# Four staging tiles for the first eight quarters of V, and six warm-up matmuls in place of eight

## The chip, the cores and the metric

One core of one Trainium2 chip. The metric is device time of one execution in microseconds (us). A run's span in the profile is about 1.7 us shorter than its time. "PE" is TensorE, "ACT" ScalarE, "DVE" VectorE, "POOL" GpSimd, "SP" the queue that issues most loads. In these traces PE runs at one of two clocks: 512-column matmuls start 0.427 us apart (the first ones of the kernel before) or 0.216 us apart (its later ones), called half clock or cold, and full clock or warm, below. The change to full clock is called the grant of the clock.

## The reference, cut to what matters

Two independent parts write the two halves of the output. Part A is a state-space layer (a complex scan over 2048 steps, 1024 states). Part B is attention over segments of 32 tokens with an 8-token memory. Only the first stage of the kernel is touched here, in which PE turns part B's input x, and multiplies it by Wv:

```python
h = jnp.concatenate([mem, xs], axis=1)          # part B, per segment
v = jnp.einsum('btd,dhe->bhte', h, Wv)          # 32 heads of 128
Bu = jnp.einsum('bld,pd->blp', x + 0j, B_bar)   # part A, "stage 1"
```

## The kernel before

PE is pinned to program order. It starts with eight matmuls on a zeroed tile, whose results are not used ("warm-ups"), while x is on its way from HBM:

```python
def warm(k, pool):
    w = pool.tile([128, 512], BF16, name="a_n", bufs=1)
    k.V.memset(w[:], 0.0)
    p = k.ps("R")
    for _ in range(8):
        k.PE.matmul(p[:], w[:, 0:128], w[:], start=True, stop=True)
```

The first quarter of V needs x turned by PE in four blocks of 128 tokens (`turn_x0`, eight 128-column transposes each, followed by a copy on DVE or ACT); the order is turn 0, turn 1, thirty-two 128-column matmuls, turn 2, and so on. Each later quarter of V is 4 x 8 matmuls of 512 columns into the three `psP` banks (tiles named ps are those that matmuls write to). ACT copies each bank into a staging tile, and when four are there, one DMA stores the tile:

```python
    def stage_init(self):
        self.vst = []
        for i in range(2):
            self.vst.append(self.wl.tile([128, 4, 4, EW], BF16, name=f"b_vst{i}", bufs=1))
            self.k.G.memset(self.vst[i][:, :, :, E:EW], 1.0)
        self.nst = 0

    def next_st(self):
        self.nst += 1
        return self.vst[self.nst % 2]

    def v_x(self, hb, q, w):
        st = self.next_st()
        # ... (first quarter: the turns and the small matmuls)
        for i in range(4):
            p = k.ps("P")[:]
            self.v_mm(p, w, 4 * q + i)
            k.copy("v" if first and i % 2 else "s", st[:, i, :, 0:E], p.rearrange("p (h e) -> p h e", h=4))
        Q.dma_start(vx[s0:s0 + n * 128, :]..., st[:, 0:n, :, :]...)      # Q = ACT's queue
```

So the copies of a quarter must wait for the store of the last quarter but one. After four quarters, "stage 1" of part A (psU<-a_xT,a_bt) is interleaved with the other quarters. `CT` is a large tile that is loaded only in stage 1's second half.

## Time and profile before

| | before |
|---|---|
| time, median of 3 | 1248.03 us (1247.3 to 1248.12) |
| span of the profiled run | 1246.5 us |
| PE busy | 1238.4 us, 99% |
| first stage-1 matmul | 36.19 us |

From the page of the kernel before (busy time of PE, and shares of the chain of waits that ended last):

```profile
span 1246.5 us, 20192 instructions
...
PE 1238.4 (99%) x8342; PEld 662.2 (53%) x8342; DVE 668.1 (54%) x1246; ACT 263.4 (21%) x631; POOL 276.5 (22%) x412
...
PE 97%; DMA 2%; ACT 1%; issue 0%; POOL 0%; DVE 0%; SPq 0%; ACTq 0%
```

PE bounds everything; a gain must be a stretch in which PE stands still or works slowly. Such stretches are read from the starts of matmuls, not from their durations: here 512-column matmuls are listed with some 0.38 us each, yet they start 0.216 us apart once warm.

The PE timeline of the kernel before; the columns are start, duration of the group, engine, line, operation, output<-inputs, count, and in brackets idle time before it and what ended it:

```profile
1.28 3.59 PE L64 MATMUL psR<-a_n 128*128 128x512 bf16 x8 [1.28 <-DVE hpb L105]
4.67 0.81 PE L64 MATMUL psU<-ident,b_xr 128*128 128x128 bf16 x8
5.93 0.62 PE L64 MATMUL psU<-ident,b_xr 128*128 128x128 bf16 x8 [0.45 <-DMA b_xr<-in_B_x_dram]
6.39 1.06 PE L64 MATMUL psP<-b_wv,b_xe 128*128 128x128 bf16 x16
7.67 1.07 PE L64 MATMUL psP<-b_wv,b_xe 128*128 128x128 bf16 x16 [0.22 <-ACT b_xe L89]
...
14.84 0.18 PE L64 MATMUL psR<-ident,a_r 24*128 24x24 bf16 x1
...
36.19 3.62 PE L64 MATMUL psU<-a_xT,a_bt 128*128 128x512 bf16 x16
```

The eight warm-ups take (4.67 - 1.28) / 8 = 0.42 us each, double the warm spacing: the array runs at half clock. The second turn waits for its load until 5.93. The single matmul at 14.84 ("a_r") ends this opening. From there to the first stage-1 matmul PE has only V matmuls.

The chain of waits of the kernel before, in order of time (start, duration, what), runs over ACT from 18.81 to 25.51 us and then over one store:

```profile
25.51 8.22 DMA b_vx<-b_vst
...
33.82 0.61 ACT b_vst L89
34.42 0.04 issue
34.47 1.89 PE psP L64 x8
```

and this is the copy that waits for that store, in the ACT timeline:

```profile
33.82 1.09 ACT L89 ACTIVATE b_vst<-psP 128x512 bf16<-128x512 f32 x2 [3.09 <-DMA b_vx<-b_vst]
```

The store of the second quarter takes 8.22 us, ACT stands 3.09 us, and PE, which has three banks to fill, at last waits too: two matmuls in a row start at 33.97 and 34.47, 0.498 us apart in place of 0.216.

### The profile page before, as it was taken

The page shows a single profiled execution, that of the slowest core. Times are in us where ns is not written, and L with a number is a line of the kernel's source. Part 1 is how long each engine was busy: PE and PEld are TensorE (multiplying, and loading weights), DVE is VectorE, ACT ScalarE, POOL GpSimd, SP SyncE. Part 2 cuts the span into 40 slices and gives each one's busy share as a digit, 9 for nine tenths or more (in the row PEclk, how much of TensorE's full clock was granted, in tenths as well). Part 3 has the DMA queues.
Part 4 walks back from the last instruction along what each step waited for, and adds up shares of the span by engine and source line. Part 5 has one row for each costly group of instructions (what it writes and reads, how often), then busy time and mean ns, then how long its engine had stood idle before and what let it go on. Part 6 is the DMA issues. An engine that isn't in the chain of part 4 may idle for free.

```text
span 1246.5 us, 20192 instructions
## 1 busy us (share of the span) xinstructions
PE 1238.4 (99%) x8342; PEld 662.2 (53%) x8342; DVE 668.1 (54%) x1246; ACT 263.4 (21%) x631; POOL 276.5 (22%) x412
## 2 busy tenths in 40 slices
PE   9999999999999999999999999999999999999998
PEld 4444444444455555656666656555665554446444
DVE  4688899998711124666666666666666641001000
ACT  5344444443310000211111111111211110000000
POOL 4111331212322321322222222222222220000000
PEclk9999999999999999999999999999999999999999
DMA  9975444554898734665454544545473279407000
GB/s 236 267 205 150 130 131 128 144 156 108 240 322 248 250 116 94 182 176 122 96 144 108 144 108 113 138 91 133 97 155 95 60 222 225 107 18 153 17 17 27
DMA packets 316023, 176.83 MB, mean 142 GB/s; under 512 B 138651, under 2 KB 301327, under 8 KB 315927
## 3 DMA queue, kind: packets, MB, share of 16 engines
q1 hardware_dynamic: 293830, 147.95, 48.4%
q10 hardware_dynamic: 21072, 24.38, 5.8%
q0 software_dynamic: 1024, 3.17, 0.7%
q8 instruction: 66, 1.08, 0.4%
q14 instruction: 31, 0.25, 0.1%
HBM read 89.14 MB, written 53.17 MB: 114 GB/s over the span
## 4 chain that ended last, share of the span: by engine, by line
PE 97%; DMA 2%; ACT 1%; issue 0%; POOL 0%; DVE 0%; SPq 0%; ACTq 0%
PE psP L64 81%; PE psU L64 9%; PE psS L64 3%; PE psO L64 2%; PE psR L64 2%; DMA wo<-in_B_Wo_dram 1%; DMA b_vx<-b_vst 1%; DMA b_xr<-in_B_x_dram 0%; ACT b_vst L89 0%; ACT L187 0%; ACT b_xe L89 0%; POOL b_m L643 0%; ACT a_fr L236 0%; ACT a_k L233 0%; ACT a_k L229 0%
## 5 line engine op out<-in xcount | busy, mean ns | idle before, releaser
L64 PE MATMUL psP<-b_xe,b_wq 128*128 128x480 bf16 (+1 forms) x1280 | 247.7, 343 | 0.0
L64 PE MATMUL psP<-b_xe,b_wk 128*128 128x480 bf16 (+1 forms) x1280 | 247.7, 343 | 0.0
L64 PE MATMUL psP<-b_wv,b_xe 128*128 128x512 bf16 (+2 forms) x1048 | 224.6, 372 | 0.3 <-ACT b_xe L89 0.2
L643 POOL TENSOR_TENSOR b_m<-b_e,maskB 99x396 bf16<-99x396 bf16 x160 | 139.6, 872 | 334.8 <-ACT b_e L640 334.8
L640 ACT ACTIVATE b_e<-psS 99x396 bf16<-99x396 f32 x176 | 88.2, 501 | 532.8 <-PE psS L64 528.5
L64 PEld LDWEIGHTS <-b_wk 128*128 128x128 bf16 x1280 | 119.4, 98 | 94.2
L64 PEld LDWEIGHTS <-b_xe 128*128 128x128 bf16 x1056 | 101.9, 98 | 119.4 <-issue 0.6
L64 PEld LDWEIGHTS <-b_wq 128*128 128x128 bf16 x1280 | 118.7, 98 | 87.7
L91 DVE CAST b_k<-psP 128x480 bf16<-128x480 f32 (+1 forms) x192 | 98.2, 533 | 100.9 <-PE psP L64 100.9
L91 DVE CAST b_q<-psP 128x480 bf16<-128x480 f32 (+1 forms) x192 | 98.2, 533 | 93.1 <-PE psP L64 91.5
L64 PEld LDWEIGHTS <-b_ol 128*128 128x128 bf16 x864 | 84.3, 98 | 94.4
L64 PE MATMUL psU<-a_xT,a_bt 128*128 128x512 bf16 x512 | 114.9, 379 | 0.0
L64 PE MATMUL psP<-t,a_hl 128*128 128x512 bf16 x512 | 113.1, 379 | 0.0
L91 DVE CAST b_ost<-psP 128x512 bf16<-128x512 f32 (+1 forms) x17 | 11.5, 676 | 183.4 <-PE psP L64 183.4
L64 PE MATMUL psP<-wo,b_ol 128*128 128x512 bf16 (+1 forms) x448 | 92.5, 364 | 0.0
L64 PE MATMUL psP<-t,b_ol 128*128 128x512 bf16 x416 | 92.2, 379 | 0.0
L280 POOL TENSOR_SCALAR a_tt<-a_pr,a_tabf 128x1 f32<-128x1 f32 x48 | 34.1, 710 | 243.5 <-DVE a_pr L275 243.5
L660 DVE TENSOR_TENSOR b_ob<-psO,b_accR 99x384 bf16<-99x384 f32 x160 | 85.9, 553 | 2.5 <-DVE b_accR L659 0.3
L89 ACT ACTIVATE b_vst<-psP 128x512 bf16<-128x512 f32 x126 | 72.1, 589 | 71.4 <-PE psP L64 60.3
L267 DVE TENSOR_TENSOR a_pr<-psU,a_tabf 128x2048 f32<-128x2048 f32 x32 | 73.0, 2283 | 14.8 <-PE psU L64 14.7
L64 PEld LDWEIGHTS <-a_bt 128*128 128x128 bf16 x512 | 49.2, 98 | 57.6
L64 PEld LDWEIGHTS <-a_hl 128*128 128x128 bf16 x512 | 49.0, 98 | 56.7
(199 smaller groups left out, 964.2 us busy)
## 6 DMA issues: line engine op xcount, KB each, us to landing
b_v<-b_vx SPq DMA_DIRECT2D x16, 1122.0 KB
b_wv<-in_B_Wv_dram SPq DMA_DIRECT2D x16, 1024.0 KB
b_on<-b_ob SPq DMA_DIRECT2D x15, 960.0 KB
b_vx<-b_vst ACTq DMA_DIRECT2D x24, 544.0 KB
a_hs<-a_h SPq DMA_DIRECT2D x32, 256.0 KB
b_wog<-in_B_Wo_dram SPq DMA_DIRECT2D x4, 2048.0 KB
b_wq<-in_B_Wq_dram SPq DMA_DIRECT2D x16, 512.0 KB
b_wk<-in_B_Wk_dram SPq DMA_DIRECT2D x16, 512.0 KB
```

The source lines that it names most:

```text
L64: r = f(*a, **kw)
L89: self.S.activation(out, in_, ACT.Copy)
L91: self.V.tensor_copy(out, in_)
L267: V.tensor_tensor(pr[:], u[:].unsqueeze(1).to_broadcast([128, 2, 2, TB]), view(t3, [[TB + 1, 2], [TB + 1, 2], [1, TB]]), ALU.mult)
L280: G.tensor_scalar(tt[:, j:j + 1], w[:, j, TB - 1:TB], t3[:, 1, TB:TB + 1], None, ALU.mult)
L640: k.S.activation(e[:], s[0:GW], ACT.Exp, scale=float(E) ** -0.5, accum_out=self.accE[0:GW, i:i + 1])
L643: k.G.tensor_tensor(m[0:GW, 0:4 * GW].rearrange("p (a b q) -> p a b q", a=2, b=2), e[:], mask[0:GW, :, :].unsqueeze(2).to_broadcast([GW, 2 ...
L660: V.tensor_tensor(self.ob[:, b0:b0 + n, :], o[0:GW, 0:n, 0:E], r.unsqueeze(2).to_broadcast([GW, n, E]), ALU.mult)
```

## The change

Intent: two further staging tiles in the space of `CT` that is not loaded yet, so that the first eight quarters do not wait for stores; and two warm-up matmuls fewer, since PE seems to warm up longer than x takes to arrive (the warm-ups run to 4.67 us; the DMA of the first block of x releases a weight load at 4.37).

```diff
-    def stage_init(self):
-        self.vst = []
-        for i in range(2):
-            self.vst.append(self.wl.tile([128, 4, 4, EW], BF16, name=f"b_vst{i}", bufs=1))
-            self.k.G.memset(self.vst[i][:, :, :, E:EW], 1.0)
+    def stage_init(self, ct):
+        self.vst = [self.wl.tile([128, 4, 4, EW], BF16, name=f"b_vst{i}", bufs=1)[:] for i in range(2)]
+        spare = [ct[:, 1, 4 * i:4 * i + 3, :].rearrange("p c d -> p (c d)")[:, 0:16 * EW].rearrange("p (i h e) -> p i h e", i=4, h=4)
+                 for i in range(2)]
+        self.sts = self.vst + spare
+        for st in self.sts:
+            self.k.G.memset(st[:, :, :, E:EW], 1.0)
         self.nst = 0
     def next_st(self):
         self.nst += 1
-        return self.vst[self.nst % 2]
+        return self.sts[self.nst % (4 if self.nst < 8 else 2)]
@@ def warm
-    for _ in range(8):
+    for _ in range(6):
         k.PE.matmul(p[:], w[:, 0:128], w[:], start=True, stop=True)
```

(Left out: the call `b.stage_init(a.CT)` and a `[:]` that moved.) The order of instructions on ACT, DVE and SP is the same in both kernels; POOL has two memsets more.

More of the change, by code (lines that the diff above doesn't have):

```diff
@@ L728, in load_o_early @@
         elif q == 2:
-            t = [v[:].rearrange("p i h e -> p (i h e)")[:, 0:2048].rearrange("p (h n) -> p h n", h=4) for v in self.vst]
+            t = [v.rearrange("p i h e -> p (i h e)")[:, 0:2048].rearrange("p (h n) -> p h n", h=4) for v in self.vst]
         else:
@@ L1008, in kernel_main @@
             b.load_m0(p1)
-            b.stage_init()
+            b.stage_init(a.CT)
             order = steps()
```

## The prediction

> **What bounds the kernel.** TensorE. The page gives PE 99% busy of a 1246.5 us span; the chain of waits is 97% PE. So the change can only pay where PE really stands still early on. From start-to-start distances in the PE timeline (a warm 512-column matmul is paced at 0.216 us) I find before 120 us just these losses: eight cold warm-up matmuls (1.28 to 4.67 us, 0.427 us each), a wait until 5.93 for the second block of x (PE waits, DMA b_xr), a wait until 7.67 for an ACT copy of x^T (0.39), and one distance of 0.498 us at 34.0, an excess of 0.285 us.
>
> **Staging tiles.** With two tiles, ACT's fourth quarter of V waits for the second quarter's store: the chain shows DMA b_vx<-b_vst from 25.51 to 33.73 (8.2 us), and the ACT timeline an idle of 3.09 us before the copy at 33.82. In the ACT group of b_vst the DMA ends 9.6 us of idle in 3 waits; another, 4.18 us, ends at 73.05. Only the first reaches PE: at 34.19 it wants a psP bank that ACT has not emptied, until 34.47. With four tiles that copy needs no store still in flight. The instruction order on ACT, DVE and SP is unchanged. So 0.285 us is gained, on the critical path, and kept: PE is paced by its own matmuls afterwards. The other ACT waits (about 6.5 us) are off the path. Added: two POOL memsets, 0.21 us each, near 5 us, ahead of an iota that DVE uses at 6.1: free. The transposed loads into CT come after 150 us, when the stores from its spare space have landed: free.
>
> **Two warm-up matmuls fewer.** They take 0.85 us, but PE then waits for data anyway. The weight load of the first transpose starts at 4.37, released by the DMA; so the first transposes could start near 4.45 instead of 4.67. That is not kept: the second ones wait for their DMA until 5.93. Gain 0. Risk: the clock. Transposes go from 0.107 to 0.056 us apart at 5.05 us, 3.77 us after PE started. [...] With six, PE is idle about 0.5 us before the first transposes; [...] the second transposes run at 0.107, delaying the ACT copy and PE by about 0.4 us. I give this one run in four: 0.1 us on average.
>
> **Sum.** 1248.03 - 0.285 + 0.1 = 1247.8 us, 0.02% faster, less than the spread of the three runs before (1247.3 to 1248.12). Range 1246.8 to 1248.8. Chances: faster by over 2% 0.003, within 2% 0.994, slower 0.003.
>
> **What would show it.** Right: ACT's 3.09 us wait gone, DMA b_vx gone from the early chain; PE's distance at 34 back to 0.216; first stage-1 matmuls near 35.9 instead of 36.19; second transposes still at 5.93 behind DMA b_xr, and 0.056 apart. Wrong: stage 1 still starts at 36.2 or later, cold transposes after 5.93, or a new wait for a store or for a_xT.
>
> **What would make it wrong.** A cold clock into the 128-column matmuls (0.5 us or more); x arriving earlier, so that fewer warm-ups pay 0.2 us or more; or a later load-bound place (8.47 us of DMA wo in the chain near 1007) absorbing the 0.285 us.

## The result, and the profile after

| | before | after |
|---|---|---|
| time, median of 4 | 1247.91 us (1247.3 to 1248.12) | 1248.89 us (1247.89 to 1249.14) |
| span of the profiled run | 1246.5 us | 1247.4 us |
| a_r matmul | 14.84 us | 16.30 us |
| first stage-1 matmul | 36.19 us | 37.37 us |

The ratio is 1.0007, 95% interval 0.999 to 1.0025: the same within 2%. (Ratios are the mean time of one kernel's fast runs over that of the other's of the same rounds, so not quite the ratio of the medians.) The four runs after were 1249.11, 1249.14, 1248.67 and 1247.89: three long, one short.

The page of the kernel after:

```profile
span 1247.4 us, 20115 instructions
...
PE 1236.0 (99%) x8268; PEld 663.4 (53%) x8340; DVE 668.2 (54%) x1246; ACT 263.5 (21%) x631; POOL 276.3 (22%) x414
...
PEclk9999999999999999999999999999999999999999
...
PE 98%; issue 0%; DMA 0%; POOL 0%; ACT 0%; DVE 0%; SPq 0%; ACTq 0%
```

The page says almost nothing: 8268 matmuls are 74 fewer than before, but only two were taken away; the others are records missing from the trace (the weight loads, PEld, are 8340 against 8342), which is also why PE's busy sum fell. Its clock row (PEclk, 9 is 90% or more) shows full speed in all 40 slices, and its mean clock is 0.999, although 128-column matmuls start 0.107 us apart until 10.3 us. The PE timeline of the kernel after tells more:

```profile
1.28 2.74 PE L64 MATMUL psR<-a_n 128*128 128x512 bf16 x6 [1.28 <-DVE hpb L105]
4.12 1.03 PE L64 MATMUL psU<-ident,b_xr 128*128 128x128 bf16 x8
5.68 1.03 PE L64 MATMUL psU<-ident,b_xr 128*128 128x128 bf16 x8 [0.53 <-DMA b_xr<-in_B_x_dram]
6.51 3.62 PE L64 MATMUL psP<-b_wv,b_xe 128*128 128x128 bf16 x32
9.92 0.80 PE L64 MATMUL psU<-ident,b_xr 128*128 128x128 bf16 x8
...
16.30 0.18 PE L64 MATMUL psR<-ident,a_r 24*128 24x24 bf16 x1
...
37.37 3.62 PE L64 MATMUL psU<-a_xT,a_bt 128*128 128x512 bf16 x16
```

The reader should look at the groups of 32 (after) and 16 + 16 (before) small V matmuls. Before, 32 take from 6.39 to 8.57 with a wait of 0.39 us within; after, 32 take from 6.51 to 9.92 with no wait: (9.92 - 6.51) / 32 = 0.107 us each against 0.056. The second turn takes 1.03 us in place of 0.62. PE is at half clock until about 10.3 us; before, until about 5.1.

The chain of waits of the kernel after has no store in its first 45 us:

```profile
1.28 4.36 DMA b_xr<-in_B_x_dram
...
5.68 1.03 PE psU L64 x8
6.72 3.41 PE psP L64 x32
...
22.23 10.77 PE psP L64 x49
```

and the ACT copy that had waited 3.09 us waits for PE alone:

```profile
32.39 0.60 ACT L89 ACTIVATE b_vst<-psP 128x512 bf16<-128x512 f32 x1 [0.20 <-PE psP L64]
```

So the span's +0.95 us (1247.42 - 1246.47) is: +1.46 up to the a_r matmul, -0.28 from there to stage 1 (21.35 us before, 21.07 after), and -0.23 over the remaining 1210 us, where both run the same work.

### The profile page after: what moved, and what is told of

Read it like the earlier page. It is cut to its first block, busy times and chain, and to the rows that moved or that the text cites. A ratio compares the mean times of both kernels' runs of the same rounds, so it can differ in the third digit from the quotient of the medians.

```text
span 1247.4 us, 20115 instructions
## 1 busy us (share of the span) xinstructions
PE 1236.0 (99%) x8268; PEld 663.4 (53%) x8340; DVE 668.2 (54%) x1246; ACT 263.5 (21%) x631; POOL 276.3 (22%) x414
## 3 DMA queue, kind: packets, MB, share of 16 engines
q0 software_dynamic: 1024, 3.17, 0.7%
## 4 chain that ended last, share of the span: by engine, by line
PE 98%; issue 0%; DMA 0%; POOL 0%; ACT 0%; DVE 0%; SPq 0%; ACTq 0%
PE psP L64 82%; PE psU L64 9%; PE psS L64 3%; PE psO L64 2%; PE psR L64 2%; DMA b_xr<-in_B_x_dram 0%; POOL b_m L645 0%; ACT b_e L642 0%; DVE b_ost L91 0%; SPq L64 0%; ACTq L89 0%; ACTq L642 0%
## 5 line engine op out<-in xcount | busy, mean ns | idle before, releaser
L89 ACT ACTIVATE b_vst<-psP 128x512 bf16<-128x512 f32 x110 | 62.9, 588 | 61.2 <-PE psP L64 57.8
```

What stands on the lines that cost most here:

```text
L89: self.S.activation(out, in_, ACT.Copy)
```

## The experiments

Theory ("window"): the staging tiles gain their 0.28 us; with six warm-ups PE idles long enough between 3.8 and 5.7 us that the full clock is granted late. Rivals: the space in CT costs something ("staging"); or the moment of the clock is luck and strikes both kernels alike ("chance").

The clock in the table below is from the trace's record of clock changes, which turn out to lie whole multiples of 3.413 us apart in these traces (from the grant to the next change 1239.04 us before, 363 of them, and 1235.63 after, 362); a "window" is such a stretch. The activity of a window is worked out from the PE timeline: each matmul counts from its start with 0.427 us per 512 columns (cold) or half of that (warm); what of this lies inside the window is summed and divided by 3.413 us. "Window before" is the 3.413 us ahead of the window that ended with the grant. Each line is one profiled run, for the clock was seen in profiled runs alone. From the first stage-1 matmul to the end all fourteen traces took 1209.86 to 1210.56 us (mean 1210.21, standard deviation 0.19), so larger differences between traces lie ahead of stage 1.

| run | warm-ups / tiles | clock granted, us | activity of window before | of the granting window | a_r, us | a_r to stage 1, us | that run, us |
|---|---|---|---|---|---|---|---|
| before | 8 / 2 | 5.08 | 11% | 100% | 14.84 | 21.35 | 1248.16 |
| after | 6 / 4 | 10.31 | 71% | 100% | 16.30 | 21.07 | 1249.11 |
| e1 | 8 / 4 | 4.10 | 0% | 83% | 14.76 | 21.07 | 1247.60 |
| e2 | 6 / 2 | 9.28 | 71% | 100% | 15.82 | 21.07 | 1248.88 |
| e3 | 6 / 4 | 4.06 | 0% | 78% | 14.38 | 21.07 | 1247.28 |
| e4 | 8 + fill / 4 | 6.86 | 64% | 100% | 15.32 | 21.07 | 1248.30 |
| e5 | 8 / 2 | 6.81 | 63% | 94% | 14.98 | 21.07 | 1247.70 |
| e6 | 8 / 2 | 4.75 | 2% | 100% | 14.89 | 21.60 | 1248.67 |
| e7 | 4 / 4 | 8.88 | 52% | 95% | 15.61 | 21.07 | 1248.45 |
| e8 | 6 + fill / 4 | 6.91 | 66% | 89% | 14.97 | 21.07 | 1248.15 |
| e9 | 8 / 4 | 5.33 | 20% | 100% | 14.57 | 21.07 | 1247.42 |
| e10 | 8 short / 4 | 3.93 | 0% | 75% | 14.84 | 21.07 | 1248.27 |
| e11 | 8 / 1 | 5.37 | 21% | 100% | 14.85 | 30.81 | 1257.65 |
| e12 | 8 / 4 | 7.30 | 77% | 82% | 15.40 | 21.07 | 1248.57 |

### e1: staging alone

```diff
 # the changed kernel, with
-    for _ in range(6):
+    for _ in range(8):
```

> Four staging tiles, but all eight warm-up matmuls. Clock theory (six warm-ups leave PE idle long enough that the clock is granted late; the staging tiles gain 0.28 us by themselves): clock granted near 5 us, the a_r matmul near 14.8 us, first stage-1 matmul near 35.9 us, time 0.3 us below before. Staging rival (the spare space in CT costs time, the warm-ups do nothing): about 1 us slower than before. Chance rival (the moment of the clock is luck in every kernel): spread of about 1.2 us like the changed kernel's, mean within 0.3 us of before.

Measured: 1247.6 us median (1247.39 to 1248.47, 5 runs), before 1247.54 (1247.47 to 1248.19, 9 runs), ratio 1.0001. Clock at 4.10, stage 1 at 35.83. The staging rival falls: with CT and eight warm-ups nothing is 1 us slower. The chance rival, that both kernels are struck alike, is not borne out by these five runs: none is as long as the long ones of the change (the count over all runs is below). But the gain of 0.3 us did not show in the time; e9 and e12 return to it.

### e2: fewer warm-ups alone

```diff
 # the kernel before, with
-    for _ in range(8):
+    for _ in range(6):
```

> Six warm-up matmuls, but two staging tiles as before. Clock theory: in most runs the clock is granted only near 8 to 10 us, the a_r matmul at up to 16.3 us; time 0.5 to 1.5 us above before, and the wait for the store is smaller or gone, since a late PE gives the store time. Staging rival: same as before within 0.2 us. Chance rival: same mean as before, single runs up to 1.5 us longer in both.

Measured: 1249.1 us median (1247.47 to 1249.72, 5 runs), before 1247.54, ratio 1.001. Four of five runs are at 1248.88 or more. The clock came at 9.28, the a_r matmul at 15.82. The whole loss is in this part of the change. The distance from a_r to stage 1 is 21.07 although there are only two tiles: PE came so late that the store was done (the ACT copy at 31.91 us waits 0.20 us, for PE). That also means that with six warm-ups the two parts of the change are not worth their sum: where the clock was late, as in this trace, four tiles had nothing left to save.

### e3: the changed kernel again

> The changed kernel once more, for the spread of its runs and a second look at the clock. Clock theory: most runs 0.8 to 1.2 us above before, a few as fast as before minus 0.3; the profile's clock is granted late (8 to 10 us) if its run is a long one and early (5 to 7 us) if it is a short one. Staging rival: always about 1 us longer, also with an early clock. Chance rival: mean equal to before.

Measured: 1247.28, 1248.83, 1248.89, 1247.52 and 1249.25 us; before 1247.54. The profile fell on the shortest. Its PE timeline:

```profile
1.28 2.74 PE L64 MATMUL psR<-a_n 128*128 128x512 bf16 x6 [1.28 <-DVE hpb L105]
3.97 0.65 PE L64 MATMUL psU<-ident,b_xr 128*128 128x128 bf16 x8
5.55 0.62 PE L64 MATMUL psU<-ident,b_xr 128*128 128x128 bf16 x8 [0.93 <-DMA b_xr<-in_B_x_dram]
6.00 1.06 PE L64 MATMUL psP<-b_wv,b_xe 128*128 128x128 bf16 x16
```

The same program, and here the first turn already runs warm (0.65 us; 1.03 in the first trace), with the clock granted at 4.06. So the kernel has two outcomes: in the nine runs of it, six at 1248.67 to 1249.25 (mean 1248.98) and three at 1247.28 to 1247.89 (mean 1247.56), 1.4 us apart. Early clock with a short run, late clock with a long one, is what the window theory said; of these nine runs the clock was seen in two.

### e4: eight warm-ups, and the wait for x filled

```diff
 # the kernel of e1, and in v_x
             self.turn_x0(0)
+            for _ in range(6):
+                k.PE.matmul(p0[:, 0:128], w0[:, 0:128], w0[:, 0:128], start=True, stop=True)
             self.turn_x0(1)
```

(`w0`, `p0` are the warm-up's operand and bank.)

> Four staging tiles, eight warm-ups, and six 128-column matmuls more between the first and the second transposes, where PE waits for x. Clock theory: no idle stretch of PE over 0.2 us before 6 us, [...] the clock is granted by 8.1 us at the latest in every run, the spread of runs is the smallest of all, time at or below that of e1 (0.3 us under before). Staging rival: about 1 us slower than before, as all with CT. Chance rival: same spread as before.

Measured: 1248.19 us median (1247.5 to 1248.35, 5 runs), before 1247.54. The clock came by 8.1, at 6.86; but neither the smallest spread nor a time under e1 was seen: a miss. In the profiled run the cold fill (0.64 us) kept PE busy until 6.16, where the second turn then started; in e1 it started at 5.66.

### e5 and e6: the kernel before, two more traces

No edit.

> The kernel before, as it is, for a second trace of it: is the wait at PE near 34 us (0.285 us for a bank that ACT has not emptied) in every run of it? Store theory [...]: the wait is there whenever the a_r matmul comes at 14.8 us or earlier, from 0.1 to 0.7 us, the distance from the a_r matmul to the first stage-1 matmul being over 21.07 us by just that. Rival (the wait of the first trace was luck): no wait, distance 21.07 us, so that four staging tiles gain nothing in most runs. Clock granted between 4.0 and 7.4 us.

> The kernel before, a third trace, for the same question as e5: under the store theory a wait of 0.1 to 0.7 us near 34 us if the a_r matmul comes by 14.8 us, under its rival none.

Measured: e5 1247.6 us median of 4 (1247.46 to 1248.15), before 1247.92; e6 a single 1248.67 us. The ACT copies that wait for the second quarter's store, e5:

```profile
32.71 1.08 ACT L89 ACTIVATE b_vst<-psP 128x512 bf16<-128x512 f32 x2 [1.83 <-DMA b_vx<-b_vst]
```

and e6:

```profile
34.12 1.08 ACT L89 ACTIVATE b_vst<-psP 128x512 bf16<-128x512 f32 x2 [3.34 <-DMA b_vx<-b_vst]
```

With the copy at 32.71 PE loses nothing (21.07 us from a_r to stage 1), with 34.12 it loses 0.54 (21.60), and with 33.82, in the first trace, 0.28. The wait at PE is real, but it is not in every run: when that store lands differs by over 1 us between runs of one program. My store theory said "whenever the a_r matmul comes at 14.8 us or earlier"; e5's came at 14.98 and so decides nothing between it and its rival, e6's came at 14.89 and shows the wait. Both clocks are within 4.0 to 7.4.

### e7: four warm-ups

```diff
 # the changed kernel, with
-    for _ in range(6):
+    for _ in range(4):
```

> Four warm-up matmuls and four staging tiles. Window theory [...]: PE is active from 1.28 to 2.99 and from 4.1 to 4.9, [...] the clock comes between 7.2 and 10.7 us in every run, all runs are over 1248.0 us, their median 1 to 1.7 us over before. Rival (the clock comes late by chance, or only the number of runs matters): some runs as short as before.

Measured: 1248.65 us median (1248.45 to 1250.1, 5 runs), before 1247.92 (1247.09 to 1248.18). Clock at 8.88, after a window of 52%. All runs are over 1248.0, as the window theory said; the median's +0.73 us is under the 1 to 1.7 that I gave, the mean's is 1249.04 - 1247.67 = 1.37. With four, no run is short; with six some are; with eight nearly all.

### e8: six warm-ups, and the wait for x filled

```diff
 # the changed kernel (six warm-ups), and in v_x
             self.turn_x0(0)
+            for _ in range(6):
+                k.PE.matmul(p0[:, 0:128], w0[:, 0:128], w0[:, 0:128], start=True, stop=True)
             self.turn_x0(1)
```

> The changed kernel (six warm-ups, four tiles) and six 128-column matmuls more between the first and the second transposes, where PE waits for x: 0.64 us of cold work put into the idle stretch, nothing else. Window theory: [...] the clock comes between 4.1 and 7.5 us, no run is as long as the long runs of the changed kernel (none over 1248.6 us), median within 0.3 us of before. Rival (what matters is the number of matmuls ahead of the first transposes, or the first transposes starting early): as the changed kernel, half the runs or more at 1248.7 to 1249.3 us.

Measured: 1248.15 us median (1247.63 to 1248.57, 5 runs), before 1247.92. The PE timeline of e8:

```profile
4.13 1.03 PE L64 MATMUL psU<-ident,b_xr 128*128 128x128 bf16 x8
4.96 0.84 PE L64 MATMUL psR<-a_n 128*128 128x128 bf16 x6
5.72 1.04 PE L64 MATMUL psU<-ident,b_xr 128*128 128x128 bf16 x8
6.55 2.39 PE L64 MATMUL psP<-b_wv,b_xe 128*128 128x128 bf16 x32
```

By luck this trace and that of the kernel after are a pair, for their windows lie almost alike. The windows that end at 3.50 us (e8) and 3.48 us (after) were 66% and 65% active, and gave no clock. In the next one the kernel after was 71% active, and got no clock at 6.89; e8, with the six matmuls in the gap, was 89% active and got it at 6.91. The fill is all that differs between the two programs. As expected no run was over 1248.6, if only just.

### e9 and e12: staging alone, for its gain

The kernel of e1, unchanged.

> Eight warm-ups and four staging tiles once more (the kernel of e1), because e1 could not tell a gain of 0.3 us from none. Two traces of before showed a wait of 0.28 and 0.54 us for the store, one showed none. Store theory: mean of the runs 0.1 to 0.4 us below before; distance from the a_r matmul to the first stage-1 matmul 21.07 us. Rival (the saved wait is given back later): same mean as before within 0.1 us, although the distance is 21.07 us. Window theory: no run over 1248.6 us.

> The kernel of e1 and e9 a third time, on the same terms as e9: store theory 0.1 to 0.4 us below before in the mean of all fifteen runs, its rival no difference within 0.1 us.

Measured: e9 1247.42 us median (1247.28 to 1247.45, 5 runs), e12 1247.57 (1247.45 to 1248.57, 5 runs), before 1247.72 (1247.16 to 1248.09, 9 runs of the same chip). All fifteen runs of this kernel have a mean of 1247.63, all 36 runs of the kernel before (e5 and e6 among them) 1247.73: 0.10 us, with a standard error of about 0.12 (standard deviations 0.39 and 0.36). The distance was 21.07 in all three traces. The saving at PE is seen in the traces: of those whose a_r matmul came before 14.9 us, the two with two tiles (before, e6) have the wait, the four with four tiles (e1, e3, e9, e10) have not. The rival "given back later" finds no support: from stage 1 to the end the three traces of before took 1210.20 us in the mean, those of e1, e9 and e12 1210.19. A gain in the time is not shown, 0.1 to 0.3 us remain possible. No run was over 1248.6, e12's longest only just under it: there the first window, begun at 0.48 us, before PE started, was 77% active and gave no clock, which came at 7.30.

### e10: eight warm-ups as short as six

```diff
 # the kernel of e1, with
-        k.PE.matmul(p[:], w[:, 0:128], w[:], start=True, stop=True)
+        k.PE.matmul(p[:, 0:384], w[:, 0:128], w[:, 0:384], start=True, stop=True)
```

> Eight warm-up matmuls of 384 columns and four staging tiles: as many matmuls as before, as much PE time (2.56 us cold) as six of 512 columns. Window theory: as the changed kernel; half the runs or more at 1248.6 to 1249.5 us with the clock at 8 to 10.7 us, the others at 1247.2 to 1248.0. Rival (the number of matmuls counts): as e1, no run over 1248.5 us.

Measured: 1248.27, 1247.13, 1247.46, 1248.82 and 1248.01 us; before 1247.72. One run is clearly long, where I expected half or more, and the profiled run of 1248.27 had its clock early (3.93), so that it is long for another reason. A miss for the window theory's number; between "time" and "number of matmuls" the run does not decide. That the number alone does not do it is seen in e8, which has six ahead of the first turn and no long run.

### e11: one staging tile

```diff
 # the kernel before, with
-        return self.vst[self.nst % 2]
+        return self.vst[1 if self.nst < 8 else self.nst % 2]
```

> Eight warm-ups and only one staging tile for the first seven quarters of V: the suspected wait made larger. Each quarter's first copy then waits for the quarter just before it to be stored (some 4 to 8 us), while three psP banks hold PE for 5.2 us. Store theory: PE stands still several times between 20 and 75 us, 3 to 15 us in all, and the whole is longer by that. Rival (the store waits are hidden by the other work, PE hardly sees them): under 1 us longer.

Measured: 1257.08 us median (1256.12 to 1259.51, 4 runs), before 1247.72, ratio 1.0078. PE's matmuls are late by 1.16, 2.64, 1.16 and 3.17 us near 21, 25, 33 and 43 us, 8.1 us together. The rival (hidden waits) falls. The rest of the 9.74 us by which the distance from a_r to stage 1 grew (30.81 against 21.07), 1.6 us, fits the clock, which was lost once more: half of the 3.40 us at clock 0.50 in the view below is 1.7. The windows view of e11, cut along multiples of 3.413 us; columns are the stretch, its length, PE's busy time and matmuls, the granted clock, DMA share and GB/s:

```profile
22.44:25.84 3.40, 0.96 (x5) 1.00 1.09 244
25.86:29.26 3.40, 3.38 (x9) 0.50 1.14 231
29.27:32.67 3.40, 3.40 (x17) 1.00 1.24 281
39.50:42.92 3.42, 1.44 (x7) 1.00 1.18 311
42.93:46.33 3.40, 2.39 (x12) 1.00 1.06 194
```

After a window with PE busy 0.96 of 3.40 us the clock is 0.50 for exactly one window, in which PE is busy all the time; then it is 1.00 again. A window with 1.44 of 3.42 did not lose it. The length of the idle stretch alone does not order the two: it was 2.48 us ahead of the matmul at 25.88, where the clock was lost, and 3.00 us ahead of the one at 43.94, where it was not.

## Why the prediction was right or wrong

- "TensorE bounds, 0.02% faster, within 2%": right that nothing moves by 2%, wrong in sign (four runs alone, with 0.999 to 1.0025, do not settle the sign; the nine runs of the kernel, mean 1248.51, against 1247.73 for before do). The median, 1248.89, is 0.09 us above the top of my range (1248.8), the point was 1.1 us too low. The second set of five runs gave 1248.83.
- "0.285 us is gained, on the critical path": the trace after has 21.07 us in place of 21.35, and its chain has lost its store; but e2, with two tiles and a late clock, has 21.07 too, so that trace does not show what the tiles did. The traces with an early a_r matmul (under e9 and e12) do. What was wrong is that I took one trace for every run: in three traces of before the wait was 0.28, 0 and 0.54. Over all runs staging is worth 0.10 us, standard error 0.12.
- "Two warm-up matmuls fewer: gain 0": right. The first turn came at 4.12 in place of 4.67, and the second waited for its load until 5.68.
- The step that failed is the risk of the clock: "the second transposes run at 0.107, delaying the ACT copy and PE by about 0.4 us. I give this one run in four: 0.1 us on average." That the clock could come late was right (10.31 us after, 5.08 before), both factors were not; one in four was my estimate, which no trace had shown. How often: of the fourteen runs with six full warm-ups (after, e2, e3) ten were long (1248.67 or more), of the 51 with eight full ones and at least two tiles (36 of before, 15 of e1, e9, e12) one, e6's, whose clock came at 4.75 and which was long by other things (below). e10, whose warm-ups took as much PE time as six, had one of five, so the share is known only roughly. How much: long and short runs of those fourteen differ by 1249.08 - 1247.54 = 1.54 us. I had counted only the second turn as cold. But in the trace after no clock came at the end of the window at 6.89; it came 3.41 us later, at 10.31, and everything up to there ran at half clock: the second turn, all 32 small V matmuls and a part of the third turn, with no wait left to hide it (before, PE stood 0.39 us at 7.67). With the clock from 8.88 to 9.28 and 10.31 the a_r matmul went from 15.61 to 15.82 and 16.30, about half a microsecond for each one. In these traces a grant by 5.4 us costs little (a_r at 14.4 to 14.9), since PE waits for x until about 5.7 anyway; one at 6.8 to 7.3 (a_r at 15.0 to 15.4) costs up to 0.6 us.
- Why six and not eight: in all fourteen traces the clock changes are whole multiples of 3.4133 us apart (362, 363 or 364 of them from the grant to the drop at the end; 6, then 1, then 359 in e11), and the grant fell anywhere from 3.9 to 10.3 us. With six warm-ups PE idles from 3.81 to 4.12 and from 4.95 to 5.68, 1.0 us (after), and a window that holds both is 71% active: no clock, twice seen (after, e2). With eight, only the gap ahead of the second turn is left, and windows that lie wholly after PE's start were 94 to 100% active, but for e12's, 82%: clock in every trace. At nearly the same place as in the kernel after, e5 (eight warm-ups, window ended at 6.81) was 94% active and got the clock. My reading is that the position of the windows decides which runs are long; that was not shown, for no run could choose it, and in unprofiled runs it was not seen. Measured: with six 10 of 14 were long, with eight 1 of 51; with four all five took 1248.45 us or more, though three of them less than 1248.67.
- Left open: what decides whether a window is followed by the clock. In these traces windows of 52 to 71% gave no clock in six (after, e2, e4, e5, e7, e8), those of 78% and more always did; between them, 75% did (e10) and 77% did not (e12), so the activity as counted here does not settle it. The profiled runs of e6 and e10 show that a time alone does not tell of a late clock: with the clock at 4.75 and 3.93 they took 1248.67 and 1248.27. In e6 0.54 us are the wait for the store; from stage 1 to the end they took 1210.47 and 1210.56 us, 0.3 more than the mean of all traces. What that 0.3 is stays open.
- A version that beats both kernels was not shown. The best choice from these runs is the staging of the change with the eight warm-ups of before: it is not slower than before (1247.63 against 1247.73, mean), and 0.9 us faster than the changed kernel (mean 1248.51 of nine); these means pool runs of several rounds and chips (within the rounds of e1 and e3 it is 1247.72 against 1248.35).

## What to carry to other kernels

Look at the idle time after the warm-up matmuls too, not only at whether they fill the time until the data comes: here, with six of them, a microsecond of idling in the opening (the trace after) went with a loss of 1.5 us in 10 of 14 runs, and with six matmuls put into the second idle stretch (e8) none of five runs was over 1248.57 us. When runs of one program fall into two groups, take several traces before explaining any of them, and compare one interior distance (here from one matmul to another) rather than the total. A buffer that ends a wait in one trace is worth that wait times the share of runs that have it.
